# Strict turns of maxima and scores in the double visits of an attention and MLP kernel, and the gate's tanh emitted behind a visit's scores

## The chip, the cores and the metric

The kernel runs on one core of one Trainium2 chip. The metric is the device time of one execution in microseconds. Three runs of the kernel before gave 1623.45, 1624.26 and 1624.90 us; the median is 1624.26 us. The profile belongs to a further execution that took 1623.24 us.

## The reference: what is computed

The input `x` is 2048 rows of 512 numbers, in float32. It is normalised by rows, and two branches use the result: attention with 32 heads of 16, and an MLP with 1792 inner units whose output passes a silu. The output is `x + s * g`.

```python
xn = _layernorm(x)
qkv = (xn @ wqkv).reshape(B, S, 3, H, Dh)
p = softmax(einsum("bhqd,bhkd->bhqk", q, k) * Dh**-0.5)
s = einsum("bhqk,bhkd->bhqd", p, v).reshape(B, S, D) @ wo
h = xn @ w1 + b1
r = where(h > 0, h, 0)
g = silu((r * r) @ w2 + b2)
out = x + s * g
```

## The kernel before, in words

**Units of work.** A unit `u` (32 of them, `NU`) is four heads by 512 queries. Each unit is walked in 16 steps `kb` of 128 keys; a step number is `st = 16 * u + kb`. One step has four *scores*, one for each head: a matmul of 64 rows into one bank of PSUM (L1225, tile `se`), and behind it an exponential on ScalarE that empties the bank into an SBUF tile (L1231, `pt` or `ex`). Two steps later `pv_step` (L1331) multiplies these tiles with the values: `pv_mm` (L380) issues four matmuls that the trace shows as eight (L382). The softmax's shift has to be known before a unit's scores, so the scores of a later unit are also computed the other way round ahead of time, and only their maxima are kept: a *maximum* is a matmul of 64 rows (L306, tile `pm_t`) and a reduction on VectorE that empties its bank (L314). Scores rotate over three banks (pool `pe`), maxima over three others (pool `pm`); the dense products have one bank (`pd`) and the product with the values one (`pv`).

**Two lanes.** Scores, maxima and the dense matmuls of the MLP and of the output projection all use 64 rows of TensorE, rows 0 to 63 (lane 0) or 64 to 127 (lane 1). The kernel writes TensorE's order by hand so that neighbours in the queue lie on different lanes and run side by side.

**Visits.** In the middle of the run, `long_slots` (L1405) handles four steps at a time. It makes two *visits*, `h = 0` and `h = 1`. In visit `h` the lane `h` works off twelve dense units (`D`; a unit is two matmuls of 256 columns in the first MLP layer, one of 512 in the second layer and in the output projection), while the other lane has maxima (`m`) and scores (`s`). `visit` (L1415) takes two strings, `mine` for lane `h` and `theirs` for the other lane, and goes through them letter by letter; the argument `h_first` says which lane's letter is queued first, and a full stop is nothing.

There are two kinds of visit, and both hold eight scores. The *single* one is cut in two: ten letters (L1459, maxima and scores in turn beside ten dense units), a `pv_step`, four letters (L1467), a second `pv_step`; it holds eight maxima. The *double* one (L1451) has fourteen letters in one piece and both `pv_step`s behind them (L1455); it holds seven maxima. `seven` (L1395) decides by the number of maxima done so far which visits are double. They come in couples, an `h = 1` visit and then the next `h = 0` visit, and couples can follow one another.

```python
visit(h, "s" + "D" * n + "s", ".mmsmssmsmssmm")   # L1451
begin(st + 1)
max_end()
shift_due()
for kb in (st - 2, st - 1):
    pv_step(kb, pts.pop(kb))
```

**What sets the order around it.** ScalarE, VectorE, GpSimd and SyncE also run in the order in which the program emits their instructions (`manual_schedule`, L1487). `begin` (L1493) sets the step number, loads what is due and calls `run_waiting` (L190), which emits every function that `later(n, fn)` (L187) has put off by `n` steps and that has come due. When a lane-1 block is finished, `visit` emits the block's `post` (L1429): for the first layer two relus on ScalarE (L554) and three operations on GpSimd (L557, L83, L84).

**The gate.** The second MLP layer is made in 8 chunks `c` of 256 tokens with two tiles `tt` each, so 16 times in all (`second`, L563). Its `post` (L574) copies the bank to `u` on ScalarE (L575), adds the bias on GpSimd (L576) and puts `gate` off by three steps (L577). `gate` (L579) is a tanh on ScalarE (L581, named `r<-u` in the trace since it writes into one of the two `r` tiles), two operations on GpSimd (L582, L583), and a store of `u` to DRAM, four steps later (L585). `gate` is emitted from `begin`, that is ahead of the visit, or between its parts.

Of the kernel before, what the change touches and what calls it, by code (L numbers as in the profile page):

```python
# [18 lines left out]
D = 512  # L19
# [9 lines left out]
NCK = S // CW  # L29
# [14 lines left out]
def kernel(  # L44
# [54 lines left out]
    with ExitStack() as ph:  # L99
# [87 lines left out]
        def later(n, fn, first=False):  # L187
            waiting.insert(0 if first else len(waiting), (now[0] + n, fn))
# [79 lines left out]
        def terms3(ps, terms):  # L268

            n = len(terms)  # L270
            out_ = []
            for t, (lh, rh) in enumerate(terms):
                for i, (a, b) in enumerate(((0, 0), (0, 1), (1, 0))):
                    out_.append((
                        ps,
                        lambda r, lh=lh, a=a: lh(a, r),
                        lambda r, rh=rh, b=b: rh(b, r),
                        t == 0 and i == 0, t == n - 1 and i == 2,
                    ))
            return out_  # L280
# [52 lines left out]
        def shift_due(slack=0):  # L333
            if late and late[0][0] + slack <= now[0]:
                shift(late.pop(0)[1])
# [32 lines left out]
                    waiting.append((16 * u - 9, back))  # L368

        in_loop = []  # L370

        def shift_rows(u, p, i):
                    nc.sync.dma_start(
                        qes[u][p].rearrange("(j r) n -> j r n", r=64)[:, 48 + i].bitcast(F32),
                        sh_d[u][16 * i + 8 * p : 16 * i + 8 * p + 8].rearrange(
                            "(j b) q -> j (b q)", j=2
                        ),
                    )
# [64 lines left out]
        def mlp_tasks(mp):  # L443
# [34 lines left out]
            def load_w2(fo, n):  # L478
                raw = ring("ex")
                nc.sync.dma_start(raw, w2[fo * P : (fo + 1) * P, :])  # L480
                later(n, lambda: split((w2t[:, 0, fo], w2t[:, 1, fo]), raw))
# [81 lines left out]
            def second(c, tt):  # L563
                hT = state["hT"]
                ps = pd.tile([P, D], F32, name="pd_t")
                u = up.tile([P, D], F32, name="u")
                th = rs[tt].rearrange("p a b -> p (a b)")
                ts_ = slice(tt * P, (tt + 1) * P)

                if c == 0 and tt == 0:  # L570
                    for k in range(5, FO):
                        later(k - 4, lambda k=k: load_w2(k, 2))

                def post():  # L574
                    nc.scalar.activation(u, ps, AF.Copy)  # L575
                    nc.gpsimd.tensor_tensor(u, u, b2_t, op=ALU.add)  # L576
                    later(3, gate)  # L577

                def gate():  # L579

                    nc.scalar.activation(th, u, AF.Tanh, scale=0.5)  # L581
                    nc.gpsimd.tensor_scalar(th, th, 0.5, 0.5, op0=ALU.mult, op1=ALU.add)  # L582
                    nc.gpsimd.tensor_tensor(u, u, th, op=ALU.mult)  # L583
                    t0 = c * CW + tt * P
                    later(4, lambda: nc.sync.dma_start(g_d[t0 : t0 + P, :], u))  # L585

                mms = terms3(ps, [
                    (lambda a, q, fo=fo: hT[q, a, fo, ts_], lambda b, q, fo=fo: w2t[q, b, fo])
                    for fo in range(FO)
                ])  # L590
                if c == 0:
                    yield from halves(mms, (6,) * 7, post, 1)
                    return
                if c == NCK - 1 and tt:

                    for i, task in enumerate(halves(mms, (6,) * 7, post, 1)):
                        if i == 4:
                            gone_pt.extend(rot["ex"])
                            free_pt[:] = [t for t in free_pt if all(t is not x for x in gone_pt)]
                        yield task  # L600
                    return

                if tt:
                    yield from halves(mms[:6], (6,), None, 1)
                    mms = mms[6:]
                for k in range(0, 36, 12):
                    yield from block(mms[k : k + 12], 1, post if tt and k == 24 else None)
                if not tt:
                    yield from halves(mms[36:], (6,), post, 1)
# [531 lines left out]
        for i in range(NT + 3):  # L1141
# [32 lines left out]
            if i >= 5:  # L1174
                rest.append(("v", (i - 3) % 4, (i - 3) // 4))
                if i % 4 == 2:
                    c = (i - 3) // 4
# [151 lines left out]
        pos = {}  # L1329

        def pv_step(st, pts):  # L1331
            u, kb = divmod(st, 16)
            if kb == 0:
                pos[0] = pv.tile([P, 512], F32, name="po")
            pv_mm(pos[0], u // 4, kb, pts)
            free_pt.extend(t for _, t in sorted(pts.items()) if all(t is not x for x in gone_pt))
            if kb == NT - 1:
                if u < NU - 2:
                    evac(pos[0], u)
                elif u == NU - 2:  # L1340
                    unit_inner(pos[0])
                else:
                    unit_final(pos[0])
# [61 lines left out]
        def long_slots(st0, units, post, wide=False):  # L1405

            todo = [[(st0 + k, j) for k in range(4) for j in (lane, lane + 2)] for lane in range(2)]
            for kb in range(st0, st0 + 4):
                pts.setdefault(kb, {})

            def s(lane):
                kb, j = todo[lane].pop(0)
                return exp_mm(kb, j, pts[kb], False)

            def visit(h, mine, theirs, h_first=False):  # L1415
                own, other, follow = units[h], 1 - h, True
                for i, ops in enumerate(zip(mine, theirs)):
                    for lane in (h, other) if h_first else (other, h):
                        o = ops[0] if lane == h else ops[1]
                        if o == "D":  # L1420
                            own.pop(0)()
                        elif o == "m":
                            max_mm(lane)
                        elif o == "s":
                            use = s(lane)
                            if lane == h and not own and follow:
                                last_use[0], follow = use, False
                    if h and not units[h] and wrap:
                        wrap.pop()()  # L1429

            wrap = [post] if post is not None else []
            for h in range(2):
                st = st0 + 2 * h
                if st > st0:
                    begin(st)
                n = len(units[h])
                if wide:
                    for i, o in enumerate("sDsDDsDDDs"):
                        for lane in range(2):
                            if o == "s":  # L1440
                                s(lane)
                            else:
                                units[lane].pop(0)()
                    if wrap and not units[0]:
                        wrap.pop()()
                    begin(st + 1)
                    shift_due()
                    for kb in (st - 2, st - 1):
                        pv_step(kb, pts.pop(kb))
                elif n == 12 and seven(st):  # L1450
                    visit(h, "s" + "D" * n + "s", ".mmsmssmsmssmm")  # L1451
                    begin(st + 1)
                    max_end()
                    shift_due()
                    for kb in (st - 2, st - 1):  # L1455
                        pv_step(kb, pts.pop(kb))
                else:
                    if n == 12:
                        visit(h, "D" * 10, "msmsmsmsms")  # L1459
                    else:  # L1460
                        visit(h, "D" * n + ".", "msmsmsmsms")
                    max_end()
                    shift_due(2 if st < 440 else 0)
                    pv_step(st - 2, pts.pop(st - 2))
                    begin(st + 1)
                    if n == 12:
                        visit(h, "DDss", "mmsm", True)  # L1467
                    else:
                        visit(h, "ss..", "mmsm", True)
                    max_end()  # L1470
                    shift_due(2 if st < 440 else 0)
                    pv_step(st - 1, pts.pop(st - 1))
            if post is not None:
                last_use[0] = None
            assert not todo[0] and not todo[1] and not units[0] and not units[1]
# [98 lines left out]
```

## Time and profile before

| | |
|---|---|
| median of three runs | 1624.26 us |
| the profiled execution, its own time | 1623.24 us |
| its span, first to last instruction | 1621.4 us |
| TensorE matmul (PE) busy | 1607.4 us, 99% |
| TensorE weight loads (PEld) busy | 963.5 us, 59% |
| VectorE (DVE) busy | 1339.5 us, 83% |
| ScalarE (ACT) busy | 1184.9 us, 73% |
| GpSimd (POOL) busy | 526.4 us, 32% |
| maxima: matmuls and reductions | 2048 of each |
| scores: matmuls and exponentials | 2048 of each |
| mean granted TensorE clock | 0.999 |

How to read it: busy time is the union of an engine's instructions, and a matmul's row covers its way through the array, so that neighbours overlap; 99% does not say that the array is full. A row of the timeline gives the start in us from the span's start, the length in us, the engine, the line, the operation, the tile written and the tiles read, the shape, how many neighbours of one kind are merged into the row, and in brackets the idle time of the engine before it and what ended it. In a merged row the length runs from the first start to the last end. A matmul that must wait does so in its weight load (PEld): that instruction carries the wait for the bank.

### The profile page before, as it was taken

What the parts mean: (1) busy time and instruction counts of PE and PEld (TensorE: products, weight loads), DVE (VectorE), ACT (ScalarE), POOL (GpSimd) and SP (SyncE); (2) the same over time, 40 slices, a digit from 0 to 9 for tenths busy, and PEclk for the clock granted to TensorE, in tenths of its full rate; (3) what the DMA queues carried; (4) which work ended last, traced back from release to release, by engine and by line L of the source; (5) the groups of instructions that cost most, each with busy time, mean ns of one, the idle gap of its engine ahead of it and who ended that gap; (6) DMA issues with size and microseconds to landing.
All of it is one profiled execution on the core that took longest, in us unless ns stands there. A gap on an engine that the chain in (4) does not pass through costs nothing.

```text
span 1621.4 us, 35371 instructions
## 1 busy us (share of the span) xinstructions
PE 1607.4 (99%) x13639; PEld 963.5 (59%) x13639; DVE 1339.5 (83%) x2327; ACT 1184.9 (73%) x2345; POOL 526.4 (32%) x549
## 2 busy tenths in 40 slices
PE   8999999999999999999999999999999999999998
PEld 6888665556556655665566556645665565554455
DVE  6499888888887888888888888888888888888833
ACT  6311777778777877777777778877877777777785
POOL 6635568223213320331132113311331133213334
PEclk9999999999999999999999999999999999999999
DMA  8895645334233631442342513333432342416443
GB/s 300 236 291 183 217 143 173 112 91 139 60 92 96 152 96 57 118 124 60 84 131 88 126 55 118 104 98 80 134 102 65 104 133 65 104 50 171 124 156 137
DMA packets 150464, 201.43 MB, mean 124 GB/s; under 512 B 50008, under 2 KB 67416, under 8 KB 148760
## 3 DMA queue, kind: packets, MB, share of 16 engines
q1 hardware_dynamic: 150296, 199.17, 41.9%
q8 instruction: 108, 1.77, 0.5%
q14 instruction: 60, 0.49, 0.1%
HBM read 144.84 MB, written 53.99 MB: 123 GB/s over the span
## 4 chain that ended last, share of the span: by engine, by line
PE 99%; DVE 0%; DMA 0%; ACT 0%; issue 0%; SPq 0%; DVEq 0%; ACTq 0%
PE po L382 31%; PE pd_t L240 18%; PE pm_t L306 17%; PE se L1225 15%; PE pd_t L208 6%; PE se L988 3%; PE se L1027 3%; PE pd_t L790 2%; PE po L1027 1%; PE pd_t L1027 1%; PE pm_t L1086 0%; PE pm_t L1225 0%; DMA xt<-in_A_x_dram 0%; PE pm_t L824 0%; PE se L872 0%; DVE mx L314 0%
## 5 line engine op out<-in xcount | busy, mean ns | idle before, releaser
L314 DVE TENSOR_REDUCE mx<-pm_t 128x1 f32<-128x512 f32 x2048 | 1266.2, 683 | 205.0 <-PE pm_t L306 111.9
L1231 ACT ACTIVATE pt<-se 128x512 f32<-128x512 f32 x1731 | 923.3, 613 | 217.9 <-PE se L1225 157.0
L306 PE MATMUL pm_t<-ka,qm 64*128 64x512 f32 x2048 | 790.0, 416 | 0.9 <-DVE mx L314 0.6
L1225 PE MATMUL se<-qe,ka 64*128 64x512 f32 x2009 | 728.4, 411 | 0.0
L382 PE MATMUL po<-pt,v 128*32 128x512 f32 x3540 | 527.9, 603 | 0.0
L306 PEld LDWEIGHTS pm_t<-ka,qm 64*128 64x128 f32 x2048 | 359.6, 184 | 219.8 <-DVE mx L314 199.5
L1225 PEld LDWEIGHTS se<-qe,ka 64*128 64x128 f32 x2009 | 349.8, 184 | 92.4 <-ACT pt L1231 63.9
L240 PEld LDWEIGHTS pd_t<-xc,w1s 64*128 64x128 f32 x2352 | 295.2, 187 | 53.0 <-issue 51.1
L240 PE MATMUL pd_t<-xc,w1s 64*128 64x256 f32 x2352 | 323.2, 286 | 0.0
L240 PE MATMUL pd_t<-w2t,hT 64*128 64x512 f32 x936 | 253.0, 406 | 0.0
L382 PE MATMUL po<-ex,v 128*32 128x512 f32 x556 | 233.9, 603 | 0.0
L1231 ACT ACTIVATE ex<-se 128x512 f32<-128x512 f32 x278 | 166.7, 614 | 49.9 <-PE se L1225 33.3
L240 PEld LDWEIGHTS pd_t<-w2t,hT 64*128 64x128 f32 x936 | 160.0, 184 | 50.5 <-issue 41.1
L382 PEld LDWEIGHTS po<-pt,v 128*32 128x32 f32 x3540 | 87.4, 108 | 150.1 <-issue 136.5
L557 POOL TENSOR_TENSOR r<-r 128x512 f32<-128x512 f32 x49 | 51.0, 1041 | 322.3 <-ACT r L554 322.3
L576 POOL TENSOR_TENSOR u<-u,b_t 128x512 f32<-128x512 f32 x16 | 20.6, 1289 | 361.3 <-ACT u L575 334.7
L208 PE MATMUL pd_t<-w2t,hT 64*128 64x512 f32 x408 | 106.0, 392 | 0.0
L208 PEld LDWEIGHTS pd_t<-w2t,hT 64*128 64x128 f32 x408 | 72.5, 184 | 10.3 <-DVE mx L314 0.7
L420 POOL TENSOR_TENSOR ot<-ot,hl 128x512 f32<-128x512 f32 x31 | 39.9, 1287 | 117.0 <-DMA hl<-r_d 86.7
L790 PE MATMUL pd_t<-wot,oc 64*128 64x512 f32 x267 | 76.1, 404 | 0.0
L84 POOL TENSOR_TENSOR hT<-r,hT 128x512 fp32r<-128x512 f32 x56 | 72.4, 1292 | 4.7
L554 ACT ACTIVATE r<-pd_t,b_t 128x256 f32<-128x256 f32 x98 | 42.2, 496 | 28.7 <-PE pd_t L240 28.7
(137 smaller groups left out, 1204.2 us busy)
## 6 DMA issues: line engine op xcount, KB each, us to landing
w1s<-w_d SPq DMA_DIRECT2D x196, 256.0 KB
xn_d<-xT SPq DMA_DIRECT2D x8, 1024.0 KB
qm<-q_d SPq DMA_DIRECT2D x128, 64.0 KB
qe<-q_d SPq DMA_DIRECT2D x128, 64.0 KB
ka<-k_d SPq DMA_DIRECT2D x32, 256.0 KB
hl<-r_d SPq DMA_DIRECT2D x31, 256.0 KB
k_d<-hl SPq DMA_DIRECT2D x30, 256.0 KB
q_d<-hl SPq DMA_DIRECT2D x15, 512.0 KB
```

What stands on the lines that cost most here:

```text
L84: (lo or nc.gpsimd).tensor_tensor(dst[1], raw, dst[0].bitcast(F32), op=ALU.subtract)
L208: mm = nc.tensor.matmul(out_, lh(r), rh(r), start=first_ and lane == 0, stop=last_ and lane == 1, skip_group_check=True,)
L240: mm = nc.tensor.matmul(out_, lh(r), rh(r), start=first_ and lane == 0, stop=last_ and lane == 1, skip_group_check=True,)
L306: nc.tensor.matmul(ps, qms[u][p][64 * j : 64 * j + 64, qb * P : (qb + 1) * P], kas[qd, p][64 * j : 64 * j + 64, kc * 512 : (kc + 1) * 512] ...
L314: return nc.vector.tensor_reduce(mxs[u][:, c, kc : kc + 1], ps, axis=AX.X, op=ALU.max)
L382: nc.tensor.matmul(po[32 * j : 32 * j + 32, :], vs[qd][:, (4 * kb + j) * VW : (4 * kb + j) * VW + 32], pts[j], start=(kb == 0), stop=(kb = ...
L557: nc.gpsimd.tensor_tensor(r, r, r, op=ALU.mult)
L790: inst = nc.tensor.matmul(ps[lane], oc[r, a, n, ts_], wot[r, b, n], start=m == 0 and (lane == 0 or wide), stop=m == kos and (lane == 1 or ...
L988: nc.tensor.matmul(out_, lh(slice(0, P)), rh(slice(0, P)), start=first_, stop=last_)
L1027: inst = nc.tensor.matmul(out_, lh(r), rh(r), start=first_ and lane == lane0, stop=last_ and lane != lane0, skip_group_check=True,)
L1225: nc.tensor.matmul(se, kas[qd, j // 2][b : b + 64, kb * P : (kb + 1) * P], qes[u][j // 2][b : b + 64, :], start=True, stop=True,)
L1231: return nc.scalar.activation(pts[j], se, AF.Exp, scale=0.25)
```

## The change

In double visits the two strings and the order of the lanes change. The other lane's letters were `.mmsmssmsmssmm`; they become `msmsmsmsmsms.m`, and lane `h`'s letter is now queued first. There are still seven maxima and eight scores, two of these on lane `h` itself, first and last letter. Each letter of the other lane thus stands in the queue behind the dense unit of the same place; before, it stood ahead of it.

The gate's instructions are no longer emitted by `run_waiting`. For the chunks 0 to 6 `gate` only puts `gate_ops` on a list `behind`, and the next `pv_step` empties the list ahead of its matmuls. The last chunk's gate is emitted as before.

```diff
+        behind = []
+
+        def run_behind():
+            while behind:
+                behind.pop(0)()
...
                 def gate():
-
+                    if c < NCK - 1:
+                        behind.append(gate_ops)
+                    else:
+                        gate_ops()
+
+                def gate_ops():
                     nc.scalar.activation(th, u, AF.Tanh, scale=0.5)
                     nc.gpsimd.tensor_scalar(th, th, 0.5, 0.5, op0=ALU.mult, op1=ALU.add)
                     nc.gpsimd.tensor_tensor(u, u, th, op=ALU.mult)
...
         def pv_step(st, pts):
+            run_behind()
             u, kb = divmod(st, 16)
...
-                    visit(h, "s" + "D" * n + "s", ".mmsmssmsmssmm")
+                    visit(h, "s" + "D" * n + "s", "msmsmsmsmsms.m", True)
                     begin(st + 1)
```

## The prediction, made before the change was run

> **What bounds the kernel now.** First the page: the busy shares and the chain that ended last.
>
> ```profile
> span 1621.4 us, 35371 instructions
> PE 1607.4 (99%) x13639; PEld 963.5 (59%) x13639; DVE 1339.5 (83%) x2327; ACT 1184.9 (73%) x2345; POOL 526.4 (32%) x549
> PE 99%; DVE 0%; DMA 0%; ACT 0%; issue 0%; SPq 0%; DVEq 0%; ACTq 0%
> ```
>
> TensorE's queue is the chain: only time that it spends waiting or filling can be won. Whom its weight loads wait for is in the list of waits (total us, times, longest):
>
> ```profile
> PEld pm_t L306 <- DVE mx L314: 199.5, 294, 0.8
> PEld se L1225 <- ACT pt L1231: 63.9, 94, 0.8
> ```
>
> The 0.8 us of the first row is the usual distance of the first load behind a product with the values, so this total isn't loss. Where loss lies is seen in one double visit. Its weight loads, the dense ones partly left out:
>
> ```profile
> 597.67 0.18 PEld L1225 LDWEIGHTS se<-qe,ka 64*128 64x128 f32 x1 [0.84 <-ACT pt L1231]
> ...
> 599.87 0.18 PEld L1225 LDWEIGHTS se<-qe,ka 64*128 64x128 f32 x1
> ...
> 600.37 0.18 PEld L1225 LDWEIGHTS se<-qe,ka 64*128 64x128 f32 x1 [0.30 <-ACT pt L1231]
> 600.37 0.18 PEld L240 LDWEIGHTS pd_t<-w2t,hT 64*128 64x128 f32 x1
> 600.47 0.19 PEld L306 LDWEIGHTS pm_t<-ka,qm 64*128 64x128 f32 x1
> ...
> 600.85 0.18 PEld L1225 LDWEIGHTS se<-qe,ka 64*128 64x128 f32 x1
> 601.27 0.11 PEld L382 LDWEIGHTS po<-ex,v 128*32 128x32 f32 x1 [0.24 <-issue]
> ```
>
> The visit lasts from 597.67 to 601.27, 3.60 us. At 600.37 a score has waited for a bank, and the dense load queued behind it, of the other lane, had to wait too. The last score loads at 600.85, and the values follow 0.42 later. Its ScalarE and VectorE:
>
> ```profile
> 598.21 0.60 ACT L1231 ACTIVATE ex<-se 128x512 f32<-128x512 f32 x1 [1.39 <-PE se L1225]
> 598.74 3.54 ACT L1231 ACTIVATE pt<-se 128x512 f32<-128x512 f32 x7
> 598.24 4.28 DVE L314 TENSOR_REDUCE mx<-pm_t 128x1 f32<-128x512 f32 x7 [1.15 <-PE se L1225]
> ```
>
> The first exponential starts 0.54 after the visit does, the second 0.53 later, and from there ScalarE has no hole: with 0.65 for the last, the pitch is (3.54 - 0.65) / 6 = 0.48. There are three banks, so the eighth score needs the fifth exponential's. That one starts at 598.74 + 3 x 0.48 = 600.18 and lasts 0.62; its end, 600.80, is 0.05 ahead of the load at 600.85. So **a double visit's length is set by ScalarE's chain of five exponentials**: first start + four pitches + 0.62 + 0.05 + 0.42. The fourth explains 600.37 in the same way.
>
> The check is a visit with a tanh in front:
>
> ```profile
> 819.07 0.18 PEld L1225 LDWEIGHTS se<-qe,ka 64*128 64x128 f32 x1 [0.84 <-ACT pt L1231]
> ...
> 822.54 0.18 PEld L1225 LDWEIGHTS se<-qe,ka 64*128 64x128 f32 x1
> 822.96 0.11 PEld L382 LDWEIGHTS po<-ex,v 128*32 128x32 f32 x1 [0.24 <-issue]
> ...
> 824.81 0.18 PEld L1225 LDWEIGHTS se<-qe,ka 64*128 64x128 f32 x1 [0.84 <-ACT pt L1231]
> ```
>
> ```profile
> 819.40 0.64 ACT L581 ACTIVATE r<-u 128x512 f32<-128x512 f32 x1
> 819.92 3.54 ACT L1231 ACTIVATE pt<-se 128x512 f32<-128x512 f32 x7
> 823.26 0.92 ACT L554 ACTIVATE r<-pd_t,b_t 128x256 f32<-128x256 f32 x2
> 823.98 0.69 ACT L1231 ACTIVATE pt<-se 128x512 f32<-128x512 f32 x1
> ```
>
> Here the first exponential starts 0.85 after the visit, the fifth ends at 819.92 + 4 x 0.48 + 0.65 = 822.49, the eighth score loads 0.05 later and the values 0.42 after that. The visit lasts 3.89.
>
> **How many.** I counted on TensorE's timeline the stretches between two products with the values that hold eight scores and seven maxima. There are 67; the first rows of the first and of the last are:
>
> ```profile
> 347.90 0.50 PE L1225 MATMUL se<-qe,ka 64*128 64x512 f32 x1
> ...
> 1543.89 0.50 PE L1225 MATMUL se<-qe,ka 64*128 64x512 f32 x1
> ```
>
> Four (at 347.90, 503.68, 819.07, 1135.01) have a tanh 0.33 after their start and last 3.89 on the mean. The other 63 last 3.60 on the mean (33 first-layer ones 3.604, 30 others 3.596).
>
> **The change part by part.** *The order of the letters.* Nothing is added or removed: seven maxima, eight scores, twelve dense units. Leaving aside the first pair (lane `h`'s first score beside the other lane's first maximum), the other lane's first score moves from its third place to its second. TensorE's steps in this visit and in a first-layer one:
>
> ```profile
> 598.47 0.39 PE L240 MATMUL pd_t<-w2t,hT 64*128 64x512 f32 x1
> ...
> 598.70 0.39 PE L240 MATMUL pd_t<-w2t,hT 64*128 64x512 f32 x1
> ```
>
> ```profile
> 520.71 0.51 PE L240 MATMUL pd_t<-xc,w1s 64*128 64x256 f32 x3
> ...
> 522.14 0.52 PE L240 MATMUL pd_t<-xc,w1s 64*128 64x256 f32 x3
> ...
> 523.65 0.41 PE L1225 MATMUL se<-qe,ka 64*128 64x512 f32 x1
> 523.99 0.62 PE L382 MATMUL po<-ex,v 128*32 128x512 f32 x2
> ```
>
> A step is 0.23. With 256 columns a dense matmul is 0.12 ((0.52 - 0.28) / 2, where 0.28 is one's length), two to a step. So the second score's matmul now starts 0.34 after the visit's start (first layer: 0.46, behind two dense ones) instead of 0.57, lasts 0.39, and is ready before ScalarE is done with the first exponential. Then the second follows at ScalarE's own pace. What that is after a hole shows a group of three whose scores are there together:
>
> ```profile
> 464.31 0.65 ACT L581 ACTIVATE r<-u 128x512 f32<-128x512 f32 x1
> 465.45 1.58 ACT L1231 ACTIVATE pt<-se 128x512 f32<-128x512 f32 x3 [0.50 <-PE se L1225]
> ...
> 467.38 0.63 ACT L1231 ACTIVATE pt<-se 128x512 f32<-128x512 f32 x1
> 469.36 1.09 ACT L1231 ACTIVATE pt<-se 128x512 f32<-128x512 f32 x2 [1.35 <-PE se L1225]
> 470.33 0.60 ACT L1231 ACTIVATE ex<-se 128x512 f32<-128x512 f32 x1
> ```
>
> From 469.36 to 470.33 are two pitches, 0.485 each. The new visit: 0.54 + 0.485 + 3 x 0.48 + 0.62 + 0.05 + 0.42 = **3.555**. The Trainium skill speaks against this term: "ScalarE: Activation LUTs" (What ACT_TABLE_LOAD costs) gives 186 ns and 0.833 ns a column, less 93 ns of overlap back to back, so 0.52 for 512 columns; with it the estimate is 0.54 + 4 x 0.52 + 0.62 + 0.05 + 0.42 = 3.71, longer than the visits are now. The rows with 0.48 decide. The ends of the term: 3.60 if the second exponential stays 0.53 behind, 3.43 if ScalarE held nothing (14 steps of 0.23 and 0.2 of fill and drain).
>
> Do the scores come in time? In a first-layer visit the score of place n starts with its second dense matmul, 0.22 + 0.24 n after the visit's start: the fifth score (place 7) at 1.90, done at 2.29; its exponential's turn is at 0.54 + 0.485 + 1.44 = 2.47. Yes, with 0.18 less the tenth that ScalarE takes to begin. The dense stream itself: 0.34 + 24 x 0.12 = 3.22 to the last score, 0.34 (523.65 to 523.99) to the values, 3.56: it ends level with ScalarE.
>
> Do the maxima? The reductions' pitch is (4.28 - 0.68) / 6 = 0.60 from 0.57 on; the third ends at 2.45, so the sixth maximum may load at 2.50. In a second-layer visit its turn would be near 2.2: it waits 0.3, and the dense load behind it (due 2.41, needed 0.11 ahead of its matmul at 2.64) just keeps its time. The seventh needs the fourth's bank, 3.10, and stands behind the last score's load at 3.13. VectorE hides, with 0.03 to spare. If that cover goes, it costs what the stop at 600.37 costs, about 0.1 a visit.
>
> Sum of this part: 63 x (3.60 - 3.555) = 2.8 us.
>
> *The tanh.* The 14 gates of chunks 0 to 6 move; the row of all 16:
>
> ```profile
> L581 ACT ACTIVATE r<-u x16: 642/643/652, 306.9 to 1452.9; 128x512 f32<-128x512 f32 x16
> ```
>
> Only the four in a double visit's front cost anything: 4 x (3.89 - 3.555) = 1.3 us. The others are covered: behind the tanh at 464.31 ScalarE idles 0.50 for lack of scores, and behind the ten letters, where this one goes, is the hole of 1.35 that takes its 0.65. Behind a double visit the eighth exponential ended at 824.67; without the tanh ahead, at about 824.35 (the visit starting as here), so the tanh, a pitch behind it, is done near 824.8. The next visit, itself 0.34 earlier, wants its first exponential at 824.81 - 0.34 + 0.54 = 825.01. It fits by 0.2. GpSimd's two operations (0.62 and 1.29, L582 and L583) now stand behind the relus' three; POOL is 32% busy, and the `r` tile that they read is written again only a slot of four steps later. The store to DRAM, on SyncE's queue, is due at the same step or one later; nothing waits for it before the next tile, over ten steps on. I price these at nothing.
>
> **Sum:** 2.8 + 1.3 = 4.1, with unrounded visit lengths 4.2 us. 1623.24 - 4.2 = 1619.0 for the profiled execution; the median of the runs is 1.02 above it, so **1620.1 us**. About 0.2% (3.2 us) is what a measurement can tell from no change here; the forecast lies only just beyond.
>
> **The rivals.** *Steps, not ScalarE, bound the visit* (chance 0.08): then second-layer visits fall to 3.43, first-layer ones stay at 3.55: 30 x 0.17 + 33 x 0.05 + 4 x 0.34 = 8.1, 1616.2 us. Against it: both visits above end on the fifth exponential to 0.01.
>
> *Scores behind dense units come too late* (0.20): the second exponential stays 0.53 behind the first, or the fifth score slips by 0.1, since each score now follows two dense matmuls of the other lane. Visits stay near 3.59: 63 x 0.01 + 4 x 0.30 = 1.8, 1622.4 us. The Trainium skill, "TensorE: Matmul & The Clock Gate" (Part 2, Step-by-step: what each phase is for), says that matmuls stay in program order and only weight loads are pulled ahead; the trace agrees as to the order (the rows' starts), and at 600.37 a load was not even pulled past a waiting one.
>
> *The tanh only changes place* (0.07): it runs into the next visit, and all moved ones in the loop (12) cost 0.3: 2.8 - 12 x 0.3 + 1.3 = 0.5, 1623.8 us. A further 0.05 is for some smaller loss that eats most of the gain.
>
> *VectorE takes over* (0.10), the slower side: in strict turn the fourth to sixth maxima ask for banks every 0.46 to 0.48 while a reduction takes 0.60, and the waiting load stops the dense stream behind it, as the score's did. It decides as soon as the bank comes over 0.03 later than worked out. Price: one more stop of 0.1 with ScalarE's chain unimproved, 63 x 0.1 - 4 x 0.19 = 5.5 slower, 1629.8 us. For it: the narrow margin; against it: the reductions' fixed pitch.
>
> **Numbers.** Forecast 0.50 (visits of 3.53 to 3.57: 1618.4 to 1621.1), rivals as above. Faster by over 0.2%: 0.50 + 0.08 = 0.58; within: 0.20 + 0.07 + 0.05 = 0.32; slower: 0.10. The range leaves out the slower rival and most of the first: 1617.4 to 1623.9.
>
> **What would show it.** Right: double visits of 3.55; the second exponential 0.49 behind the first; no stop of 0.30 before a score's load late in the visit, so of the 94 waits on `pt` some 60 gone; each moved tanh behind an eighth exponential, in front of a hole. Wrong: stops before maxima's loads within the visit (VectorE), a fifth exponential with idle time in front (late scores), a first exponential over 0.6 after the visit's start (tanh). A changed number of double visits would upset the whole sum.

## The result and the profile after

The changed kernel takes 1621.3 us (median of 15 runs, 1620.09 to 1622.03) against 1624.2 us (15 runs, 1623.45 to 1626.01): 2.9 us or 0.18% faster, ratio 0.9982 with a 95% interval of 0.9974 to 0.9989. The forecast was 1620.1 us. The profiled execution took 1621.41 us.

The page of the changed kernel, and two rows of its list of waits; from line 371 on the lines have moved (scores are L1235, exponentials L1241, products with the values L387, the tanh L591):

```profile
span 1619.4 us, 35369 instructions
PE 1605.3 (99%) x13639; PEld 963.0 (59%) x13639; DVE 1339.8 (83%) x2327; ACT 1183.4 (73%) x2345; POOL 524.8 (32%) x549
PE 99%; DVE 0%; ACT 0%; DMA 0%; issue 0%; POOL 0%; DVEq 0%; SPq 0%; ACTq 0%
```

```profile
PEld pm_t L306 <- DVE mx L314: 199.5, 292, 0.8
...
PEld se L1235 <- ACT pt L1241: 63.1, 91, 0.8
```

The same visit as in the prediction, now at 596.96; its weight loads and its ScalarE:

```profile
596.96 0.18 PEld L1235 LDWEIGHTS se<-qe,ka 64*128 64x128 f32 x1 [0.84 <-ACT pt L1241]
...
599.47 0.18 PEld L306 LDWEIGHTS pm_t<-ka,qm 64*128 64x128 f32 x1
599.47 0.18 PEld L240 LDWEIGHTS pd_t<-w2t,hT 64*128 64x128 f32 x1
599.61 0.18 PEld L1235 LDWEIGHTS se<-qe,ka 64*128 64x128 f32 x1
...
600.10 0.18 PEld L1235 LDWEIGHTS se<-qe,ka 64*128 64x128 f32 x1 [0.30 <-ACT pt L1241]
600.10 0.18 PEld L306 LDWEIGHTS pm_t<-ka,qm 64*128 64x128 f32 x1
600.53 0.11 PEld L387 LDWEIGHTS po<-ex,v 128*32 128x32 f32 x1 [0.25 <-issue]
```

```profile
597.49 0.60 ACT L1241 ACTIVATE ex<-se 128x512 f32<-128x512 f32 x1 [1.40 <-PE pm_t L306]
597.99 3.53 ACT L1241 ACTIVATE pt<-se 128x512 f32<-128x512 f32 x7
```

The second exponential starts 0.50 behind the first; before it was 0.53. The visit lasts 3.57 instead of 3.60. The stop of 0.30 on a score's bank has not gone: it stood 0.9 ahead of the values and held a dense load up; now it stands in front of the last score, when TensorE has only the last maximum left. That fits a visit whose end is set by ScalarE. The list has 91 waits of scores where it had 94, but it is no count of such stops: 60 of the 91 (61 of the 94) are the 0.84 at the start of a double visit, behind the product with the values. Inside double visits it has 24 stops, all in front of the eighth and last score (6 more of the kind are listed under the tile `ex`); before it had 25, all in front of the seventh.

A visit that had a tanh in front, now without it, and the tanh behind:

```profile
818.46 0.18 PEld L1235 LDWEIGHTS se<-qe,ka 64*128 64x128 f32 x1 [0.84 <-ACT pt L1241]
...
822.04 0.11 PEld L387 LDWEIGHTS po<-ex,v 128*32 128x32 f32 x1 [0.24 <-issue]
...
823.89 0.18 PEld L1235 LDWEIGHTS se<-qe,ka 64*128 64x128 f32 x1 [0.84 <-ACT pt L1241]
```

```profile
822.35 0.90 ACT L559 ACTIVATE r<-pd_t,b_t 128x256 f32<-128x256 f32 x2
823.07 0.67 ACT L1241 ACTIVATE pt<-se 128x512 f32<-128x512 f32 x1
823.54 0.71 ACT L591 ACTIVATE r<-u 128x512 f32<-128x512 f32 x1
824.42 0.60 ACT L1241 ACTIVATE pt<-se 128x512 f32<-128x512 f32 x1 [0.17 <-PE pm_t L306]
```

3.58 instead of 3.89. The tanh ends at 824.25, and the next visit's first exponential, 0.53 after that visit's start, finds ScalarE idle for 0.17.

I summed the 67 double visits on TensorE's timeline as for the prediction, in every profile (the number stayed 67). The last column is the span less that sum: the rest of the kernel. "Against before" is the median less that of the kernel before on the same chip.

| kernel | median us | against before | 67 visits, us | rest of the span |
|---|---|---|---|---|
| before | 1624.2 | | 242.4 | 1379.0 |
| changed | 1621.3 | -2.9 | 239.7 | 1379.7 |
| again | 1621.32 | -2.89 | 239.7 | 1378.9 |
| e1_order_only | 1622.58 | -1.63 | 241.0 | 1378.6 |
| e2_gate_only | 1623.02 | -1.19 | 241.4 | 1379.8 |
| e3_early_score | 1621.12 | -3.09 | 239.5 | 1379.7 |
| e4_late_score | 1623.79 | -0.19 | 242.4 | 1378.3 |
| e5_other_first | 1623.70 | -0.28 | 241.9 | 1379.5 |
| e6_half_exp | 1618.77 | -5.21 | 237.0 | 1379.2 |
| e7_vector_85 | 1621.00 | -2.98 | 239.7 | 1379.0 |
| e8_vector_reduce | 1626.64 | +2.84 | 245.2 | 1379.7 |

The visits explain every row to 0.3 us. The rest wanders by 0.8 to either side with no relation to the edit, so that one pair of profiles alone (1621.4 and 1619.4) would have shown only 2.0 us. Two executions at a low granted clock, one of e1 (2561.64 us at 0.595) and one of the kernel before beside it (1918.24 us at 0.753), are in the medians, which they move by at most 0.02 us, and not in the ratios.

### The profile page after: what moved, and what is told of

Read it like the earlier page. It is cut to its first block, busy times and chain, and to the rows that moved or that the text cites. A ratio compares the mean times of both kernels' runs of the same rounds, so it can differ in the third digit from the quotient of the medians.

```text
span 1619.4 us, 35369 instructions
## 1 busy us (share of the span) xinstructions
PE 1605.3 (99%) x13639; PEld 963.0 (59%) x13639; DVE 1339.8 (83%) x2327; ACT 1183.4 (73%) x2345; POOL 524.8 (32%) x549
## 4 chain that ended last, share of the span: by engine, by line
PE 99%; DVE 0%; ACT 0%; DMA 0%; issue 0%; POOL 0%; DVEq 0%; SPq 0%; ACTq 0%
PE po L387 31%; PE pd_t L240 18%; PE pm_t L306 17%; PE se L1235 15%; PE pd_t L208 6%; PE se L998 3%; PE se L1037 3%; PE pd_t L800 2%; PE po L1037 1%; PE pd_t L1037 1%; PE pm_t L1096 0%; PE pm_t L1235 0%; DVE mx L314 0%; PE pm_t L834 0%; PE se L882 0%; DMA wv<-in_A_wqkv_dram 0%
## 5 line engine op out<-in xcount | busy, mean ns | idle before, releaser
L1241 ACT ACTIVATE pt<-se 128x512 f32<-128x512 f32 x1731 | 923.3, 616 | 217.3 <-PE se L1235 149.3
L306 PE MATMUL pm_t<-ka,qm 64*128 64x512 f32 x2048 | 826.5, 423 | 1.2 <-DVE mx L314 0.9
L1235 PE MATMUL se<-qe,ka 64*128 64x512 f32 x2009 | 717.4, 407 | 0.0
L387 PE MATMUL po<-pt,v 128*32 128x512 f32 x3540 | 527.9, 603 | 0.0
L306 PEld LDWEIGHTS pm_t<-ka,qm 64*128 64x128 f32 x2048 | 364.2, 184 | 222.1 <-DVE mx L314 199.5
L1235 PEld LDWEIGHTS se<-qe,ka 64*128 64x128 f32 x2009 | 345.2, 184 | 89.0 <-ACT pt L1241 63.1
L240 PE MATMUL pd_t<-xc,w1s 64*128 64x256 f32 x2352 | 319.6, 285 | 0.0
L240 PE MATMUL pd_t<-w2t,hT 64*128 64x512 f32 x936 | 248.2, 402 | 0.0
L387 PE MATMUL po<-ex,v 128*32 128x512 f32 x556 | 234.0, 603 | 0.0
L1241 ACT ACTIVATE ex<-se 128x512 f32<-128x512 f32 x278 | 167.7, 618 | 50.5 <-PE se L1235 32.4
L387 PEld LDWEIGHTS po<-pt,v 128*32 128x32 f32 x3540 | 87.4, 108 | 150.5 <-issue 137.4
L208 PE MATMUL pd_t<-w2t,hT 64*128 64x512 f32 x408 | 106.0, 392 | 0.0
```

The costliest lines, as they stand in the source:

```text
L208: mm = nc.tensor.matmul(out_, lh(r), rh(r), start=first_ and lane == 0, stop=last_ and lane == 1, skip_group_check=True,)
L240: mm = nc.tensor.matmul(out_, lh(r), rh(r), start=first_ and lane == 0, stop=last_ and lane == 1, skip_group_check=True,)
L306: nc.tensor.matmul(ps, qms[u][p][64 * j : 64 * j + 64, qb * P : (qb + 1) * P], kas[qd, p][64 * j : 64 * j + 64, kc * 512 : (kc + 1) * 512] ...
L387: nc.tensor.matmul(po[32 * j : 32 * j + 32, :], vs[qd][:, (4 * kb + j) * VW : (4 * kb + j) * VW + 32], pts[j], start=(kb == 0), stop=(kb = ...
L1235: nc.tensor.matmul(se, kas[qd, j // 2][b : b + 64, kb * P : (kb + 1) * P], qes[u][j // 2][b : b + 64, :], start=True, stop=True,)
L1241: return nc.scalar.activation(pts[j], se, AF.Exp, scale=0.25)
```

## The experiments

Theory A is the prediction's: a double visit ends a fixed 0.48 behind the end of the fifth exponential. Rival B: the strict turns win because the late pair of scores no longer stops the dense stream. Rival C: only the tanh's place counts.

**The changed kernel again, and its two halves.** `again` is the changed kernel without an edit.

> The changed kernel once more, beside the kernel before on the same chip. Theory A (a double visit's length is set by ScalarE's first five exponentials: first start 0.53 to 0.54, four pitches, the fifth's length, 0.05 and 0.43): double visits of 3.57 us, the fifth exponential ending near 3.09, about 2.7 us less than before in all, near 1621.5 us. If the 0.7 us by which the profiled executions differ less than their double visits is a cost of the change (GpSimd, SyncE), the rest of the profile is 0.7 us longer again; if it is spread, it is not.

Measured 1621.32 us, ratio 0.9984 (0.9975 to 0.9993). Its rest of the span is that of the kernel before, so the moved work on GpSimd and SyncE costs nothing that shows above the 0.8 by which the rest wanders.

`e1_order_only`, the kernel before with one line changed:

```diff
-                    visit(h, "s" + "D" * n + "s", ".mmsmssmsmssmm")
+                    visit(h, "s" + "D" * n + "s", "msmsmsmsmsms.m", True)
```

> The new strings alone, the gate emitted as before. Theory A: the 63 visits without a tanh fall from 3.60 to 3.57, the four with one stay at 3.89, since behind a tanh the second exponential follows the first at 0.48 already: 63 x 0.027 = 1.7 us faster, 1622.5 us. Rival C (only the tanh's place counts): no change, 1624.2 us.

Measured 1622.58 us, ratio 0.9990 (0.9981 to 0.9999); the 63 visits last 3.576 on the mean, the four with a tanh 3.90 to 3.97. Rival C falls, since the order alone gains. ScalarE in one of the four:

```profile
503.46 0.64 ACT L581 ACTIVATE r<-u 128x512 f32<-128x512 f32 x1
503.98 0.61 ACT L1231 ACTIVATE pt<-se 128x512 f32<-128x512 f32 x1
504.46 0.62 ACT L1231 ACTIVATE ex<-se 128x512 f32<-128x512 f32 x1
504.94 1.12 ACT L1231 ACTIVATE pt<-se 128x512 f32<-128x512 f32 x2
505.89 0.65 ACT L1231 ACTIVATE ex<-se 128x512 f32<-128x512 f32 x1
```

The first two exponentials are 0.48 apart with either order, so the order has nothing to give here. The rows also show that a back-to-back exponential lasts longer the further back it stands (0.61, 0.62, fifth 0.65) while the starts stay 0.48 apart.

`e2_gate_only` is the changed kernel with that line set back.

> The gate behind the scores alone, the strings as before. Theory A: the four visits with a tanh fall from 3.89 to 3.60, the others stay at 3.60: 4 x 0.29 = 1.2 us faster, 1623.0 us. If the tanh only changes place, its 0.64 us shows as a later first exponential in the visit behind and nothing is won: 1624.2 us.

Measured 1623.02 us, ratio 0.9993 (0.9984 to 1.0002); no visit is longer than 3.64, the mean is 3.603. The interval just reaches 1, but the sum of visits is 1.0 us smaller, and the two halves add up (1.63 + 1.19 = 2.82 against 2.89).

**Strict turns, or an early second exponential?** `e3_early_score` keeps the old order and swaps two letters; `e4_late_score` does the reverse to the new one. Both have the gate of the changed kernel.

```diff
-                    visit(h, "s" + "D" * n + "s", "msmsmsmsmsms.m", True)
+                    visit(h, "s" + "D" * n + "s", ".msmmssmsmssmm")          # e3
+                    visit(h, "s" + "D" * n + "s", "mmssmsmsmsms.m", True)    # e4
```

> The gate as in the changed kernel, the strings of before with only the other lane's second and third letters swapped, so that its first score stands one place earlier; the late pair of scores in a row stays, and so does the stop in front of it. Theory A: the second exponential starts 0.49 behind the first, visits of 3.57 to 3.58, as fast as the changed kernel, near 1621.5 us. Rival B (the strict turns win, because the late pair of scores no longer stops the dense stream): visits stay at 3.60, 1623.0 us.

Measured 1621.12 us, ratio 0.9982 (0.9973 to 0.9991). The weight loads of the same visit, scores only:

```profile
599.07 0.18 PEld L1235 LDWEIGHTS se<-qe,ka 64*128 64x128 f32 x1
599.56 0.18 PEld L1235 LDWEIGHTS se<-qe,ka 64*128 64x128 f32 x1 [0.27 <-ACT pt L1241]
600.05 0.18 PEld L1235 LDWEIGHTS se<-qe,ka 64*128 64x128 f32 x1
600.48 0.11 PEld L387 LDWEIGHTS po<-ex,v 128*32 128x32 f32 x1 [0.25 <-issue]
```

The visit began at 596.91, so it lasts 3.57. The stop in front of the seventh score is still there (599.56), no strict turns anywhere, and the whole gain is had: rival B falls.

> The changed kernel with the other lane's second and third letters swapped (m m s s m s ...): strict turns from the fifth letter on, dense units first, but the other lane's first score one place later. Theory A: the second exponential is again 0.53 behind the first, visits of 3.61, 1623.5 to 1624 us. Rival B (strict turns): the end of the visit is in strict turn without a stop, visits stay at 3.57, near 1621.5 us.

Measured 1623.79 us, ratio 0.9997 (0.9989 to 1.0006), mean visit 3.617. ScalarE in the same visit, which began at 597.00:

```profile
597.54 0.60 ACT L1241 ACTIVATE ex<-se 128x512 f32<-128x512 f32 x1 [1.40 <-PE pm_t L306]
598.08 3.53 ACT L1241 ACTIVATE pt<-se 128x512 f32<-128x512 f32 x7
```

0.54 between the first two, and the order's gain is gone although the end is in strict turn.

**Whose letter is queued first.** `e5_other_first` is the changed kernel without the last argument:

```diff
-                    visit(h, "s" + "D" * n + "s", "msmsmsmsmsms.m", True)
+                    visit(h, "s" + "D" * n + "s", "msmsmsmsmsms.m")
```

> The changed kernel with the other lane's letter queued ahead of the dense unit again. Theory A: scores are no later than in the changed kernel, visits of 3.57, no difference from it, near 1621.5 us. If putting the dense unit first matters by itself, visits differ from 3.57 by more than 0.02 in the first-layer visits.

Measured 1623.70 us, ratio 0.9999 (0.9990 to 1.0008), visits of 3.61: the expectation missed. The visit that began at 597.77:

```profile
598.34 0.60 ACT L1241 ACTIVATE ex<-se 128x512 f32<-128x512 f32 x1 [1.44 <-PE se L1235]
598.83 3.54 ACT L1241 ACTIVATE pt<-se 128x512 f32<-128x512 f32 x7
```

```profile
598.30 4.28 DVE L314 TENSOR_REDUCE mx<-pm_t 128x1 f32<-128x512 f32 x7 [1.19 <-PE se L1235]
```

The second exponential is 0.49 behind the first, as it should be, but the first starts 0.57 after the visit instead of 0.53, and the reduction 0.53 instead of 0.57. Of the two matmuls that open a visit side by side, the reader of the one queued second starts 0.03 to 0.04 later. In the changed kernel that is the maximum's reader, here the score's. "TensorE: Matmul & The Clock Gate" of the Trainium skill (The cost: per-tile semaphore tail) has the semaphore increments of concurrent matmuls go one behind another, 26.3 ns each; the 0.03 to 0.04 here is of that size, somewhat longer, and no run isolated the increment. Theory A's sum with this start gives the measured visit; what I had missed is that its first term depends on the order.

**What stands next to ScalarE.** `e6_half_exp` halves the columns of the exponentials in double visits (a row falls from 0.60 to 0.38), `e7_vector_85` and `e8_vector_reduce` add to VectorE's work. In the lines below, `half[0]` is true only while a double visit's letters are emitted, `many` is 128x64 of a constant tile, and the last two lines belong to one run each.

```diff
+            w = 256 if half[0] else 512                                                   # e6
-            return nc.scalar.activation(pts[j], se, AF.Exp, scale=0.25)
+            return nc.scalar.activation(pts[j][:, :w], se[:, :w], AF.Exp, scale=0.25)
...
                             max_mm(lane)
+                            if len(mine) == 14 and i == 2:
+                                nc.vector.memset(idle, 0.0)                               # e7
+                                nc.vector.tensor_reduce(idle[:, :16], many, axis=AX.X, op=ALU.max)  # e8
```

> The changed kernel with the exponentials of double visits working on 256 of the 512 columns only (half of each tile is left as it was). Theory A: ScalarE stops being the bound and the next ones show, VectorE's fourth reduction (end 3.05, hence 3.53) and in first-layer visits the dense stream (3.53 to 3.56): visits of 3.50 to 3.56, 1 to 5 us faster than the changed kernel. If ScalarE isn't the bound, visits stay at 3.57.

Measured 1618.77 us, ratio 0.9970 (0.9957 to 0.9983); all visits lie between 3.527 and 3.546. In one that began at 595.22 the reductions, and the loads of the last score and the last maximum:

```profile
595.80 4.28 DVE L314 TENSOR_REDUCE mx<-pm_t 128x1 f32<-128x512 f32 x7 [1.11 <-PE pm_t L306]
```

```profile
598.10 0.18 PEld L1236 LDWEIGHTS se<-qe,ka 64*128 64x128 f32 x1
598.34 0.18 PEld L306 LDWEIGHTS pm_t<-ka,qm 64*128 64x128 f32 x1
598.76 0.11 PEld L387 LDWEIGHTS po<-ex,v 128*32 128x32 f32 x1 [0.24 <-issue]
```

With a pitch of 0.60 and a length of 0.68 the fourth reduction ends at 595.80 + 1.80 + 0.68 = 598.28, 0.06 ahead of the maximum's load, while the last score had loaded 0.24 earlier. So VectorE is the next bound, only 0.04 below ScalarE.

> The changed kernel with one small memset on VectorE (128x32, 85 ns in the profile before) behind the second maximum of each double visit. It measures how far VectorE is from the bound. Theory A: the fourth reduction ends near 3.14 instead of 3.05, the last maximum loads at 3.19 instead of 3.15: visits of 3.61 to 3.62, 67 x 0.04 = 3 us slower than the changed kernel. If VectorE had more than 0.1 in hand, visits stay at 3.57.

Measured 1621.00 us, no difference: a second miss, of the probe rather than of the theory. The memset did not hold VectorE up by its length:

```profile
432.61 0.09 DVE L1437 MEMSET idle<- 128x32 f32 x1
432.61 3.04 DVE L314 TENSOR_REDUCE mx<-pm_t 128x1 f32<-128x512 f32 x5
```

Both rows begin at 432.61: the reduction's row overlaps with it, and the chain of reductions moved by only 0.01 (the fourth ends 3.067 after a visit's start on the median, in the changed kernel 3.054). A reduction of 128x64 does move it:

> The changed kernel with one more reduction of 128x64 on VectorE behind the second maximum of each double visit; in the profiles so far such a one moves what follows it by 0.126 us, where the memset tried before moved it by 0.01. Theory A (ScalarE's fifth exponential ends the visit, VectorE's fourth reduction only 0.04 behind it): the fourth reduction ends at 3.18 instead of 3.06, the last maximum loads at 3.23, visits of 3.66: 67 x 0.09 = 6 us slower than the changed kernel, near 1627 us. If VectorE has more than 0.13 in hand, visits stay at 3.57 and the time near 1621.3 us.

Measured 1626.64 us, ratio 1.0016 (1.0007 to 1.0026), mean visit 3.660. The visit that began at 599.61:

```profile
601.38 0.21 DVE L1438 TENSOR_REDUCE idle<-ident 128x16 f32<-128x64 f32 x1
601.51 3.07 DVE L314 TENSOR_REDUCE mx<-pm_t 128x1 f32<-128x512 f32 x5
```

```profile
602.24 0.18 PEld L306 LDWEIGHTS pm_t<-ka,qm 64*128 64x128 f32 x1 [0.28 <-DVE mx L314]
602.75 0.18 PEld L1237 LDWEIGHTS se<-qe,ka 64*128 64x128 f32 x1 [0.21 <-ACT pt L1243]
602.84 0.18 PEld L306 LDWEIGHTS pm_t<-ka,qm 64*128 64x128 f32 x1
603.26 0.11 PEld L387 LDWEIGHTS po<-ex,v 128*32 128x32 f32 x1 [0.24 <-issue]
```

The last maximum loads 3.23 after the visit's start and ends it 0.42 later; a stop in front of a maximum's load (602.24) is new. The last score still stops for ScalarE (602.75), but for 0.21 instead of 0.30, and it no longer ends the visit: the last maximum, 0.09 behind it, does. The fourth reduction ends 0.125 later than in the changed kernel and the visits grow by 0.082, so VectorE had 0.04 in hand, as by e6. This is the mechanism of the prediction's slower rival, brought about by added work.

## Why the prediction was right, and where it was off

- **What bounds the visit** was right: e3, e4 and e5 change the letters or the queue's order in three ways, and in each the visit's end goes with the starts of the first two exponentials; e6 frees it by taking ScalarE's work away.
- **The order's term** (2.8 us) had the right mechanism and was sized twice too large: it gave 1.4 us by the visits (63 x (3.600 - 3.578)) and 1.63 us by e1. The step that was mis-sized is "0.54 + 0.485 + 3 x 0.48 + 0.62 + 0.05 + 0.42 = 3.555". The starts were right (the fifth exponential's near 2.46). Its length was not: I took 0.62 from the visit of before, where the late second exponential had broken the run; in an unbroken run it stands one place further back and lasts 0.63, and the tail was 0.43. Typical visits are 3.573, so the sum was 0.018 short where the whole forecast gain is 0.045 a visit. By ends the working is shorter: in the changed kernel the ends of successive exponentials lie 0.49 apart up to the fifth (medians 0.488 to 0.490), so the fifth ends at 0.535 + 0.598 + 4 x 0.49 = 3.09, and the last score loads 0.05 later.
- **Four visits of 3.64 to 3.65** I had not foreseen (0.3 us). In them the last maximum, now queued behind the last score, loads 0.07 later than that score, where elsewhere it follows at once. In all four, and in no other double visit of this kernel, TensorE's queue holds between the two an instruction of 51 ns that waits for the semaphores of DMA transfers. In the visit at 637.07 the same instruction stood before the change 2.67 after the start, ahead of the last score, and that visit (then at 637.84) lasted 3.573.
- **The tanh's term** (1.3 us) was right: 4 x (3.892 - 3.578) = 1.3, and 1.19 us by e2. Its cover behind the visit was estimated at 0.2 and shows as the 0.17 of idle time. GpSimd and SyncE at nothing was right too, as far as the wandering rest can tell.
- **VectorE close behind** was right, 0.03 by the working and 0.04 by e6 and e8. So was the first-layer dense stream, level with it: in e6's first-layer visits the last score loads 3.094 after the start, its bank free since the fifth exponential's end at 2.63, and the last maximum at 3.108. What the steps alone would give a second-layer visit (3.43 in the prediction) no run shows, since VectorE ends them at 3.54.
- **The sum** was 4.2 us, the result 2.9: right in sign, inside the range, and 0.2 us outside the interval of 1618.4 to 1621.1 that I gave even odds. At 0.18% it lies within the 0.2% that I called hard to tell from no change; fifteen runs of each told it. By the number alone the result, 1621.3, lies about halfway between the forecast, 1620.1, and the rival of late scores, 1622.4. The second exponential decides between them: that rival keeps it 0.53 behind the first, and it came 0.494 behind on the median; where it comes 0.53 to 0.54 behind (e4), the order's gain is gone.
- **What would show it** was wrong in one point: I expected the stop of 0.30 late in the visit, and with it some 60 of the 94 waits of scores, to go. The 60 were misread: as many are the waits at the visits' starts, which no order of letters touches. The stop itself moved to the last score in the 30 visits that are not of the first layer; here the wait for the engine that sets the pace moved and did not vanish.
- By "ScalarE: Activation LUTs" of the Trainium skill (What ACT_TABLE_LOAD costs) the visit would have come to 3.71; the trace disagrees, with starts 0.48 apart in a run where the page's figures give 0.52.

## What to carry to other kernels

When an engine drains a ring of n banks, work out which of its outputs frees the bank for the last producer and add up the drainer's work to the end of that one; in these visits the pattern in between mattered only through the first two. Put the first two producers as early as they go, and the one that feeds the slower chain ahead in the queue: here swapping two letters did all that the new order does. When a change frees the bound, look at how far off the next ones stand before hoping for more: VectorE was 0.04 us behind, less than one edit's error.

## What the runs showed of the hardware that was not expected

- Exponentials of 128x512 back to back start 0.48 us apart but last longer by about 0.012 each (0.61, 0.62, ... 0.65 for the fifth), and the load that waits for the bank comes 0.05 behind the end. A hole in the run sets the length back to about 0.60. Their ends lie 0.49 apart either way: in e3's first-layer visits the fifth starts 2.489 after the visit and lasts 0.606, in the changed kernel 2.458 and 0.632, and both end near 3.09.
- Two matmuls that start side by side on the two lanes release their readers 0.03 to 0.04 us apart, in the order of the queue.
- A 128x32 memset on VectorE between two large reductions moved those behind it by 0.01 (e7), a 128x64 reduction by 0.13 (e8).
